# Other halves and other engines for the split of q and k, in an attention and expert kernel

## The chip, the cores and the metric

The kernel runs on one core of one Trainium2 chip. The metric is the device time of one execution, in microseconds (us). A core has five engines that run side by side, each with a queue of its own that it works off in order: TensorE (PE, with its weight loads shown as PEld), VectorE (DVE), ScalarE (ACT), GpSimd (POOL) and SyncE (SP), which here only issues DMAs. An instruction that waits holds up everything behind it in its queue.

## The reference

Eight batches of eight heads of causal attention with a bias that grows with the distance, and then a layer of eight experts, of which each token takes the best one:

```python
scores = scale * np.matmul(q, k.transpose(0, 1, 3, 2))          # 8, 8, 576, 64
cum = np.cumsum(np.maximum(s, 0.0), axis=-1)
bias = -(cum[:, :, :, None] - cum[:, :, None, :])
scores = np.where(causal, -1000000000.0, scores + np.minimum(bias, 0.0))
attn = softmax(scores);  x = (attn @ v), as 4608 tokens x 512
logits = x @ w_gate + modality_bias[modality_id];  e_idx = argmax(logits)
for e in range(E):                                               # 8 experts
    h = np.maximum(x[e_idx == e] @ w1[e], 0.0)                   # 512 -> 1024
    out[e_idx == e] = gate_w[...] * (h @ w2[e])                  # 1024 -> 512
```

## The kernel before

*Pairs.* The attention runs over 32 pairs: one head in two batches (`ab` or `a` = 0 and 1). Eight pairs make a group, which holds all heads of two batches. q and k lie transposed, 64 rows of the head's dimension, and the host writes each of them twice, into partitions 0 to 63 and 64 to 127.

*The split of q and k.* Matmuls run on `F32R`, which keeps fewer bits than float32, so q and k are cut into a high part (the value cast to `F32R`) and a low part (what is left). A score is two matmuls into one tile `sp`: line 288 multiplies `QH` (q's high part in both halves of the partitions) with `KA` (k's high part in one half and its low part in the other), and line 289 multiplies `QL` with `KB`: q's low part with k's high part in partitions 0 to 63, and in further partitions the bias, as rows that `place` brings in by DMA.

*Preparing a pair* (`prep`, lines 223 to 251) is a generator, advanced once in each step of the pair before. Before the change POOL makes the high parts `QH`, `KA` and `KB` (line 233), KA's low part in partitions 64 to 127 (line 248) and QL for `a` = 1 (line 250), DVE makes QL for `a` = 0 (line 239). The first pair has a version of its own, `prep0`.

*A step.* `run` goes through nine steps in a pair, for items in the order 3, 7, 2, 6, 8, 1, 5, 0, 4. Items 0 to 3 are the query blocks of the first batch, of 128 to 512 keys, 4 to 7 those of the second, and 8 holds the last 64 queries of both. A step issues an item's score on PE, its minimum with the mask on DVE (line 291, or 305 for item 8), the exponential on ACT (line 311), and, three steps later, the transposes on PE (line 321) with the copy of the result into `PT` on ACT (line 324) or, for the items in `PTDVE`, on DVE (line 340). The transposes have two buffers, `pt`. `tail` multiplies `PT` with v (`o`, line 361), copies `o` to `oT` on ACT and DVE (lines 364 and 368), multiplies with the gate's weights beside an identity (`ox`, line 255) and scales into `x` and `xq` on DVE (lines 383 and 385).

*Between.* After a group, `Route.group` finds each token's expert on DVE, and POOL scatters nine blocks of rows into `lists` by indirect DMA (line 610), one every `SCS` steps. The third group also computes the first tables of the expert stage. At steps of `setup` constants are written and the bias rows `ek` and `eq` are saved to memory (`save`), from where the pairs from 8 on load them. Each pair's step 7 loads q, k and v of the pair after the next; the buffers are two for q and k, three for v. A planner orders the instructions by their place in the program and by when it thinks them ready; `issue_after` puts an instruction behind another on its engine.

*After.* The expert stage works on blocks of 256 tokens, with weights split in the same way.

Of the kernel before, what the change touches and what calls it, by code (L numbers as in the profile page):

```python
# [7 lines left out]
F32 = mybir.dt.float32  # L8
# [3 lines left out]
AF = mybir.ActivationFunctionType  # L12
ALU = mybir.AluOpType
# [4 lines left out]
P = 128  # L18
KW = 576
XW = 72  # L20
# [7 lines left out]
SPB = 4  # L28
PTDVE = (8,)
QUIET = (6, 7, 8)  # L30


class Attn:

    def __init__(self, ctx, tc, qkv, s, ident):
# [34 lines left out]
        zz = t1.tile([P, 1], F32, name="zz")  # L72
        nc.vector.memset(zz, 0.0)
        for c in range(4):
            nc.vector.memset(ek.bitcast(F32)[:, c, P * (c + 1):], 0.0)
        ho = self.hot(t1)
        nc.vector.tensor_scalar(sr, sr, 0.0, 8.0, ALU.max, ALU.mult)
        cum = [self.ps1.tile([P, 512], F32, name="sp", bufs=SPB) for _ in range(2)]
        nc.vector.tensor_tensor_scan(cum[0], sr[:, :512], zz.broadcast_to([P, 512]), 0.0, ALU.add, ALU.add)
        nc.vector.tensor_tensor_scan(cum[1][:, :64], sr[:, 512:], zz.broadcast_to([P, 64]), cum[0][:, 511:512], ALU.add, ALU.add)  # L80
        nb = t1.tile([P, 5], F32, name="nb")
        nc.vector.tensor_scalar(nb[:, :4], cum[0][:, 0:512:P], -1.0, None, ALU.mult)
        nc.vector.tensor_scalar(nb[:, 4:], cum[1][:, :1], -1.0, None, ALU.mult)
        ekf = ek.bitcast(F32)
        up = slice(64, P)
        for c in (3, 2, 1, 4, 0):
            n = min(P * (c + 1), KW)
            with self.tc.issue_after(self.act):
                for g in range(2 if c == 4 else 1):
                    k = slice(512 * g, min(n, 512 * g + 512))  # L90
                    w = k.stop - k.start
                    i = nc.scalar.activation(ek[:, c, k], cum[g][:, :w], AF.Identity, bias=nb[:, c:c + 1])
                    lo = nc.vector.scalar_tensor_tensor(ek[up, c, k], cum[g][up, :w], nb[up, c:c + 1], ekf[up, c, k], ALU.add, ALU.subtract)
        self.act = i.ins
        with self.tc.issue_after(self.act):
            self.prep0(raw, 0)

        dg = ekf.rearrange("p c k -> p (c k)")
        with self.tc.issue_after(self.act), self.tc.issue_after(lo.ins):
            for ab in range(2):  # L100
                copy = nc.scalar.copy if ab else nc.vector.tensor_copy
                for u in range(2):
                    r = slice(64 * u + 32 * ab, 64 * u + 32 * ab + 32)
                    copy(eq[r, 64 * ab:64 * ab + 512].rearrange("p (c q) -> p c q", c=4),
                         dg[r, :2816].rearrange("p (c x) -> p c x", c=4)[:, :, :P])
                    copy(eq[r, 512 * (1 - ab):512 * (1 - ab) + 64], dg[r, 2816:])
            self.prep0(raw, 1)
            self.rows(ho, 1)
        for pi in range(2):
            self.place(pi)  # L110

    def save(self):

        nc = self.nc
        self.ekd = self.dr.tile([64, 2, 5 * KW], F32, name="ekd")
        self.eqd = self.dr.tile([64, 2, KW], F32, name="eqd")
        for u in range(2):
            r = slice(64 * u, 64 * u + 64)
            nc.sync.dma_start(self.ekd[:, u], self.ek.bitcast(F32)[r].rearrange("p c k -> p (c k)"))
            nc.sync.dma_start(self.eqd[:, u], self.eq.bitcast(F32)[r])  # L120

    def hot(self, t1):

        nc = self.nc
# [8 lines left out]
        self.rows(ho, 0)  # L133
        with self.tc.issue_after(i.ins):
# [18 lines left out]
    def prep0(self, raw, part):  # L153

        nc = self.nc
        rq, rk = raw
        QH, QL, KA, KB = self.QH[0], self.QL[0], self.KA[0], self.KB[0]
        QHf, KAf = QH.bitcast(F32), KA.bitcast(F32)
        lo, up = slice(0, 64), slice(64, P)
        if part:  # L160
            nc.scalar.copy(QH[:, 1, :KW], rq[:, 1])
            nc.scalar.copy(KB[lo, 1], rk[lo, 1])
# [6 lines left out]
        nc.scalar.copy(KA[:, 1], rk[:, 1])  # L169
        nc.scalar.copy(KB[lo, 0], rk[lo, 0])  # L170
        self.last = nc.gpsimd.tensor_tensor(KA[up, 1], rk[up, 1], KAf[up, 1], ALU.subtract).ins

# [21 lines left out]
    def consts(self):  # L194
        nc = self.nc
        for u in range(2):
            nc.gpsimd.memset(self.oT[u][:, 512:], 0.0)
        for t in self.PT:
            nc.vector.memset(t[64:, PTW - 64:], 0.0)
        nc.gpsimd.memset(self.pw, 0.0)  # L200
        for ab in range(2):
            rows = slice(64 * ab, 64 * ab + 64)
            idv = self.ident[rows, 64 * ab:64 * ab + 64]
            nc.scalar.copy(self.pw[rows, :, XW * ab:XW * ab + 64], idv.unsqueeze(1).broadcast_to([64, 8, 64]))
            nc.scalar.copy(self.pq[rows, :, :64], idv.unsqueeze(1).broadcast_to([64, 8, 64]))

# [11 lines left out]

    def load(self, pi):
        self.raw[pi] = self.load_qk(pi)  # L220
        self.V[pi] = self.load_v(pi)

    def prep(self, pi):
        nc = self.nc
        rq, rk = self.raw.pop(pi)
        QH, QL, KA, KB = (t[pi % 2] for t in (self.QH, self.QL, self.KA, self.KB))
        QHf, KAf = QH.bitcast(F32), KA.bitcast(F32)
        if pi > 1:
            self.place(pi)

        def high(o, i):
            with self.tc.issue_after(self.last):
                self.last = nc.gpsimd.tensor_scalar(o, i, 1.0, 1.0, ALU.mult, ALU.mult).ins  # L233

        lo, up = slice(0, 64), slice(64, P)
        for a in range(2):
            high(QH[:, a, :KW], rq[:, a])
        with self.tc.issue_after(self.hold[0]):
            nc.vector.tensor_tensor(QL[lo, 0, :KW], rq[lo, 0], QHf[lo, 0, :KW], ALU.subtract)
        yield  # L240
        for a in range(2):
            high(KA[:, a], rk[:, a])
        yield
        for a in range(2):
            high(KB[lo, a], rk[lo, a])
            yield
        for a in range(2):
            self.last = nc.gpsimd.tensor_tensor(KA[up, a], rk[up, a], KAf[up, a], ALU.subtract).ins  # L248
            yield
        self.last = nc.gpsimd.tensor_tensor(QL[lo, 1, :KW], rq[lo, 1], QHf[lo, 1, :KW], ALU.subtract).ins  # L250
        yield

# [135 lines left out]
    def run(self, npair, newx, done, setup):  # L388
# [5 lines left out]
        for k in range(n + LAG + 9):  # L394
            if k < n:
# [38 lines left out]
def pack(q, k, v, s):  # L434
# [17 lines left out]
    ss = s.reshape(4, 2, 8, 576).transpose(1, 0, 2, 3).reshape(64, 576)  # L452
    return np.ascontiguousarray(out), np.ascontiguousarray(ss)

# [7 lines left out]
PRI2 = 250  # L462
SCS, XB = 4, 4
NRA, NRB = 2, 4
# [8 lines left out]
class Route:  # L473
# [83 lines left out]
    def group(self, bp, x, psum, mm, then=None):  # L557
# [51 lines left out]
        for t in range(9):  # L609
# [4 lines left out]
            self.scat.append(i)  # L614
            for _ in range(SCS):
                yield False
# [393 lines left out]
def build(tc, qkv, s, mid, wg, mb, w1, w2, out):  # L1010
    nc = tc.nc
    with ExitStack() as ctx:
# [9 lines left out]
        with ExitStack() as actx:  # L1022
            xps = [xctx.enter_context(tc.tile_pool(name="xp0", bufs=2, side="right"))]
            A = Attn(actx, tc, qkv, s, ident)

# [77 lines left out]
```

## Time and profile before

| | us |
|---|---|
| median of 3 runs | 898.26 (897.01 to 899.95) |
| the profiled execution | 901.84 |
| its span, first to last instruction | 900.1 |

| engine | busy us | share of the span |
|---|---|---|
| PE | 833.4 | 93% |
| PEld | 726.4 | 81% |
| DVE | 633.0 | 70% |
| ACT | 527.3 | 59% |
| POOL | 574.1 | 64% |

The mean granted clock of TensorE is 0.970. Attention ends at about 427 us, and the rest is the expert stage. The profile's rows give line, engine, operation and tiles as output<-inputs, partitions x elements, a count, busy us and mean ns of one, then the idle time of the engine just before these instructions and what ended it. A row of waits says who waited for whom: us in total, times, longest. A row of the timeline begins with start and duration in us, and its bracket gives the idle time just before and what ended it. POOL's spans are rough, and ends of matmuls are modelled.

### The profile page before, as it was taken

The numbers are of one execution on the slowest core, as the hardware profiler recorded it, in microseconds if no ns is written. First come the engines' busy times: TensorE is split into PE (matmuls) and PEld (weight loads), VectorE is DVE, ScalarE is ACT, GpSimd is POOL, SyncE is SP. The second block draws the span as 40 slices with busy tenths as digits, with TensorE's granted clock in tenths as the row PEclk, the third lists the DMA queues.
The fourth block names the chain that finished last, engine by engine and source line by source line (L and its number), as shares of the span: only waits on it lengthen the run. The fifth ranks groups of instructions, "written<-read, shape, count | busy, mean of one in ns | idle before, by whom it ended". The sixth has DMA issues, their size and how long they took to land. (4 is left out here: it accounts for less than half of the span.)

```text
span 900.1 us, 16902 instructions
## 1 busy us (share of the span) xinstructions
PE 833.4 (93%) x5648; PEld 726.4 (81%) x5648; DVE 633.0 (70%) x1543; ACT 527.3 (59%) x1221; POOL 574.1 (64%) x471
## 2 busy tenths in 40 slices
PE   2889999997999899898989799999999999999984
PEld 2778888876887688686889698999999999999962
DVE  7668788877878688967748866666665666656681
ACT  5757888775877577677545244455554544444541
POOL 7767777778768787772556256565555655545860
PEclk9989999998999899989999999999999999999987
DMA  4563444534445444534878376666666666665840
GB/s 166 162 170 120 161 140 141 186 120 163 140 167 161 142 140 141 191 107 165 312 265 309 133 271 230 238 234 237 237 236 237 237 237 237 237 235 220 294 160 3
DMA packets 68888, 172.85 MB, mean 192 GB/s; under 512 B 13247, under 2 KB 13247, under 8 KB 68672
## 3 DMA queue, kind: packets, MB, share of 16 engines
q1 hardware_dynamic: 62944, 151.70, 48.8%
q0 software_dynamic: 5856, 20.06, 5.7%
q8 instruction: 45, 0.74, 0.3%
q14 instruction: 43, 0.35, 0.1%
HBM read 144.75 MB, written 26.80 MB: 191 GB/s over the span
## 5 line engine op out<-in xcount | busy, mean ns | idle before, releaser
L311 ACT ACTIVATE pe<-pe,mx 128x512 f32<-128x512 f32 (+3 forms) x256 | 143.5, 563 | 29.7 <-DVE mx L291 28.1
L291 DVE CUSTOM_DVE_ANT_0 pe<-sp,mk 128x512 f32<-128x512 f32 (+3 forms) x256 | 120.8, 485 | 28.1 <-PE sp L289 26.4
L324 ACT COPY PT<-pt 128x512 f32<-128x512 f32 (+3 forms) x256 | 104.4, 420 | 53.1 <-PE pt L321 50.1
L907 ACT ACTIVATE hT<-hp 128x512 fp32r<-128x512 f32 x72 | 42.8, 594 | 151.7 <-PE hp L905 147.9
L891 POOL DMA_INDIRECT out<-ys,oi x36 | 40.8, 1133 | 131.8 <-DVE ys L890 49.8
L321 PE MATMUL pt<-ident,pe 128*128 128x128 f32 x640 | 120.3, 287 | 1.5 <-ACT PT L324 1.5
L288 PE MATMUL sp<-KA,QH 128*128 128x256 f32 (+2 forms) x256 | 105.7, 416 | 15.2 <-POOL KA L168 10.4
L361 PE MATMUL o<-PT,V 128*64 128x320 f32 (+4 forms) x896 | 109.7, 373 | 3.5 <-DVE PT L340 3.4
L361 PEld LDWEIGHTS o<-PT,V 128*64 128x64 f32 x896 | 81.7, 140 | 36.4 <-DVE PT L340 15.8
L248 POOL TENSOR_TENSOR KA<-rawk,KA 64x576 fp32r<-64x576 f32 x62 | 88.0, 1434 | 24.9 <-DMA lists<-x,di 19.1
L905 PE MATMUL hp<-xT,wcb 128*128 128x256 f32 x648 | 90.0, 283 | 0.9 <-DVE hT L908 0.9
L321 PEld LDWEIGHTS pt<-ident,pe 128*128 128x128 f32 x640 | 78.9, 147 | 13.3 <-issue 5.6
L289 PE MATMUL sp<-KB,QL 76*128 76x256 f32 (+2 forms) x256 | 88.3, 347 | 0.8 <-POOL QL L250 0.7
L908 DVE SCALAR_TENSOR_TENSOR hT<-hp,hT 128x512 fp32r<-128x512 f32 x72 | 49.3, 684 | 53.0 <-ACT hT L907 52.9
L905 PEld LDWEIGHTS hp<-xT,wcb 128*128 128x128 f32 x648 | 83.5, 189 | 1.7 <-DVE hT L908 1.1
L905 PE MATMUL hp<-xT,wcc 128*128 128x256 f32 x528 | 76.5, 286 | 5.5 <-DVE hT L908 3.1
L884 PE MATMUL y<-wcb,hT 128*128 128x512 f32 x336 | 81.0, 398 | 0.0
L233 POOL TENSOR_SCALAR QH<-rawq 128x576 fp32r<-128x576 f32 x62 | 41.2, 682 | 60.5 <-issue 42.5
L905 PE MATMUL hp<-xT,wca 128*128 128x256 f32 x552 | 78.4, 285 | 0.4 <-ACT xT L870 0.3
L905 PEld LDWEIGHTS hp<-xT,wcc 128*128 128x128 f32 x528 | 69.6, 193 | 6.6 <-DVE hT L908 3.3
L884 PEld LDWEIGHTS y<-wcb,hT 128*128 128x128 f32 x336 | 62.9, 189 | 14.6
L905 PEld LDWEIGHTS hp<-xT,wca 128*128 128x128 f32 x552 | 72.2, 191 | 1.3 <-ACT xT L870 0.5
(271 smaller groups left out, 1952.4 us busy)
## 6 DMA issues: line engine op xcount, KB each, us to landing
wrbw<-in_w SPq DMA_DIRECT2D x104, 512.0 KB
wraw<-in_w SPq DMA_DIRECT2D x56, 512.0 KB
rawq<-in_qkv SPq DMA_DIRECT2D x32, 576.0 KB
rawk<-in_qkv SPq DMA_DIRECT2D x32, 576.0 KB
xg<-lists SPq DMA_DIRECT2D x18, 576.0 KB
V<-in_qkv SPq DMA_DIRECT2D x32, 320.0 KB
lists<-z SPq DMA_DIRECT2D x8, 576.0 KB
ekd<-ek SPq DMA_DIRECT2D x2, 720.0 KB
```

The costliest lines, as they stand in the source:

```text
L248: self.last = nc.gpsimd.tensor_tensor(KA[up, a], rk[up, a], KAf[up, a], ALU.subtract).ins
L288: self.pe.append(nc.tensor.matmul(sp[:, :nn], QH[:, q0:q0 + P], KA[:, ab, :nn], start=True, stop=False).ins)
L289: self.pe.append(nc.tensor.matmul(sp[:, :nn], QL[:EXT, q0:q0 + P], KB[:EXT, ab, :nn], start=False, stop=True).ins)
L291: ins = nc.vector.tensor_tensor_reduce(out=t[:, :n], in0=sp[:, :n], in1=self.mk[:, 512 - n:512], scale=-0.125, scalar=3.0e38, op0=ALU.add, ...
L311: self.act = nc.scalar.activation(t[:, :n], t[:, :n], AF.Exp, bias=m, scale=-1.0, accum_out=st["sums"][:, o:o + 1]).ins
L321: self.pe.append(nc.tensor.transpose(out=pt[:, P * j:P * j + P], in_=pe[:, P * j:P * j + P], identity=self.ident).ins)
L324: cp(w[:, :, v:v + P], pt[:, :P * (c + 1)].rearrange("p (j q) -> p j q", q=P))
L361: m = nc.tensor.matmul(o[r, f - q0:q1 - q0], V[:, ab, j, :], PT[ab][:, PTS * j + f if j < 4 else PTW - 64:PTS * j + q1 if j < 4 else PTW], ...
L884: self.last[0] = nc.tensor.matmul(y[u], hT[:, a, f, P * u:P * u + P], W[4 + f // 2][:, c, 512 * (f % 2):512 * (f % 2) + 512], start=f == 0 ...
L905: nc.tensor.matmul(hp[:, u], W[k][:, a, f:f + P], xT[:, c, k], start=k == 0 and i == 0, stop=k == 3 and i == 2)
L907: nc.scalar.activation(hs, hp, AF.Relu)
L908: nc.vector.scalar_tensor_tensor(hT[:, 1, 2 * m:2 * m + 2], hp, 0.0, hs.bitcast(F32), ALU.max, ALU.subtract)
```

## The change

- `prep`: KA's conversion for both `a` goes from POOL to ACT, behind the latest exponential. KA's low part goes from partitions 64 to 127 into 0 to 63 (the high part stands in the other half, so the products are the same), and both low parts of q are made on POOL. The order is now QH, KB, QL, and KA last.
- `PTDVE` is (2, 6, 8) in place of (8): the copies of items 2 and 6 go from ACT to DVE.
- `SCS` is 5 for the first two groups and stays 4 for the others.
- v of a pair is loaded at step 2 of the pair before; before, it was loaded five steps and a whole pair earlier, at step 7. `save` writes the halves at steps 17 and 26 and no longer both at 17.
- The start: `s` comes doubled from the host in one DMA; ACT does its maximum and scale, in two parts; the scan is in three parts; ACT copies the upper half of the sums into a tile `cl`, from which DVE makes the low parts of `ek`; all of the first pair's KA is made on POOL; the rows `eq` are all copied by ACT; `pw` and `pq` (identity and gate's weights) are filled at the start and no longer at steps 5 and 8.

```diff
-PTDVE = (8,)
+PTDVE = (2, 6, 8)
-SCS, XB = 4, 4
+SCS = 5, 5, 4, 4
...
     def __init__(self, ctx, tc, qkv, s, ident, wg):
-        for u in range(2):
-            nc.sync.dma_start(sr[64 * u:64 * u + 64], s)
+        nc.sync.dma_start(sr, s)
         raw = self.load_qk(0)
-        self.load(1)
-        self.V[0] = self.load_v(0)
+        self.raw[1] = self.load_qk(1)
+        for pi in range(2):
+            self.V[pi] = self.load_v(pi)
...
-        nc.vector.tensor_scalar(sr, sr, 0.0, 8.0, ALU.max, ALU.mult)
+        nc.vector.memset(self.pw, 0.0)
+        self.unit(self.pq, 0)
+        self.setup(wg)
+        for k in (slice(0, 256), slice(256, KW)):
+            i = nc.scalar.activation(s8[:, k], sr[:, k], AF.Relu, scale=8.0)
+        with self.tc.issue_after(i.ins):
+            self.rows(ho, 0)
...
+        cl = self.ps1.tile([P, 512], F32, name="pt")
+        with self.tc.issue_after(self.act):
+            i = nc.scalar.copy(cl[up], cum[0][up])
+        self.act = i.ins
...
-                    lo = nc.vector.scalar_tensor_tensor(ek[up, c, k], cum[g][up, :w], ...)
+                    lo = nc.vector.scalar_tensor_tensor(ek[up, c, k], (cum[1] if g else cl)[up, :w], ...)
...
+        own(0, 0); own(0, 1)                      # eq's rows, all on ACT
+        for ab in range(2):
+            own(1, ab)
+            self.prep0(raw, 1 + ab)               # KB on ACT, QL on DVE
+        self.place(0)
+        self.rows(ho, 1)
+        self.unit(self.pw, XW)
+        self.place(1)
...
+    def unit(self, t, w):
+        for ab in range(2):
+            rows = slice(64 * ab, 64 * ab + 64)
+            self.act = self.nc.scalar.copy(t[rows, :, w * ab:w * ab + 64], self.ident[rows, 64 * ab:64 * ab + 64]...).ins
...
     def prep0(self, raw, part):
-        nc.gpsimd.tensor_scalar(QH[:, 0, :KW], rq[:, 0], 1.0, 1.0, ALU.mult, ALU.mult)
-        nc.gpsimd.tensor_scalar(KA[:, 0], rk[:, 0], 1.0, 1.0, ALU.mult, ALU.mult)
-        nc.gpsimd.tensor_tensor(KA[up, 0], rk[up, 0], KAf[up, 0], ALU.subtract)
-        nc.scalar.copy(KA[:, 1], rk[:, 1])
...
+        for a in range(2):
+            nc.gpsimd.tensor_scalar(QH[:, a, :KW], rq[:, a], 1.0, 1.0, ALU.mult, ALU.mult)
+            nc.gpsimd.tensor_scalar(KA[:, a], rk[:, a], 1.0, 1.0, ALU.mult, ALU.mult)
+            self.last = nc.gpsimd.tensor_tensor(KA[lo, a], rk[lo, a], KAf[lo, a], ALU.subtract).ins
...
     def prep(self, pi):
+        def low(o, i, h):
+            with self.tc.issue_after(self.last):
+                self.last = nc.gpsimd.tensor_tensor(o, i, h, ALU.subtract).ins
         for a in range(2):
             high(QH[:, a, :KW], rq[:, a])
-        with self.tc.issue_after(self.hold[0]):
-            nc.vector.tensor_tensor(QL[lo, 0, :KW], rq[lo, 0], QHf[lo, 0, :KW], ALU.subtract)
-        yield
-        for a in range(2):
-            high(KA[:, a], rk[:, a])
         yield
         for a in range(2):
             high(KB[lo, a], rk[lo, a])
+        yield
+        for a in range(2):
+            low(QL[lo, a, :KW], rq[lo, a], QHf[lo, a, :KW])
             yield
         for a in range(2):
-            self.last = nc.gpsimd.tensor_tensor(KA[up, a], rk[up, a], KAf[up, a], ALU.subtract).ins
+            with self.tc.issue_after(self.act):
+                self.act = nc.scalar.copy(KA[:, a], rk[:, a]).ins
+            low(KA[lo, a], rk[lo, a], KAf[lo, a])
             yield
-        self.last = nc.gpsimd.tensor_tensor(QL[lo, 1, :KW], rq[lo, 1], QHf[lo, 1, :KW], ALU.subtract).ins
-        yield
...
     def run(self, npair, newx, done, setup):
+                if k % 9 == 2 and 0 < pi < npair - 1:
+                    self.V[pi + 1] = self.load_v(pi + 1)
                 if k % 9 == 7 and pi + 2 < npair:
-                    self.load(pi + 2)
+                    self.raw[pi + 2] = self.load_qk(pi + 2)
...
-            for _ in range(SCS):
+            for _ in range(SCS[bp]):
                 yield False
...
-            setup = {5: A.consts, 7: R.consts, 8: lambda: A.setup(wg), 17: A.save, 20: lambda: R.setup(mid, mb, A.t1p)}
+            setup = {5: A.consts, 7: R.consts, 17: lambda: A.save(0), 26: lambda: A.save(1), 20: lambda: R.setup(mid, mb, A.t1p)}
```

More of the change, by code (lines that the diff above doesn't have):

```diff
@@ L28, with __init__ @@
 SPB = 4
-PTDVE = (8,)
+PTDVE = (2, 6, 8)
 QUIET = (6, 7, 8)
 class Attn:
-    def __init__(self, ctx, tc, qkv, s, ident):
+    def __init__(self, ctx, tc, qkv, s, ident, wg):
         nc = tc.nc
@@ L109, in __init__ @@
-        for pi in range(2):
-            self.place(pi)
-    def save(self):
-        nc = self.nc
[L115 to L120, printed above, removed]
+                    lo = nc.vector.scalar_tensor_tensor(ek[up, c, k], (cum[1] if g else cl)[up, :w], nb[up, c:c + 1], ekf[up, c, k], ALU.add, ALU.subtract)
@@ new lines, in __init__, with own @@
+            self.act = i.ins
+        self.prep0(raw, 0)
+        dg = ekf.rearrange("p c k -> p (c k)")
+        up = slice(64, P)
+        def own(u, ab):
+            with self.tc.issue_after(self.act):
+                r = slice(64 * u + 32 * ab, 64 * u + 32 * ab + 32)
+                nc.scalar.copy(eq[r, 64 * ab:64 * ab + 512].rearrange("p (c q) -> p c q", c=4),
+                               dg[r, :2816].rearrange("p (c x) -> p c x", c=4)[:, :, :P])
+                self.act = nc.scalar.copy(eq[r, 512 * (1 - ab):512 * (1 - ab) + 64], dg[r, 2816:]).ins
@@ new lines, in __init__ @@
+        own(0, 0)
+        own(0, 1)
+        self.hold[0] = lo.ins
+        for ab in range(2):
+            own(1, ab)
+            with self.tc.issue_after(self.act), self.tc.issue_after(self.hold[0]):
+                self.prep0(raw, 1 + ab)
+        self.place(0)
+        with self.tc.issue_after(self.act):
+            self.rows(ho, 1)
+        with self.tc.issue_after(self.act):
+            self.unit(self.pw, XW)
[3 more added lines that the diff above has]
+            rows = slice(64 * ab, 64 * ab + 64)
+            self.act = self.nc.scalar.copy(t[rows, :, w * ab:w * ab + 64], self.ident[rows, 64 * ab:64 * ab + 64].unsqueeze(1).broadcast_to([64, 8, 64])).ins
@@ L199, in consts @@
             nc.vector.memset(t[64:, PTW - 64:], 0.0)
[L200 to L205, printed above, removed]
     def load_qk(self, pi):
```

49 lines of the change are left out of this document (21 added, 28 removed).

## The prediction

> **What bounds the kernel now.** I read the stages first (busy time by stretch), then the time of each pair of heads, then the waits, then the instructions around the longest waits. The first row below shows all engines from pair 4 to pair 11 (us, busy us and count of PE, PEld, DVE, ACT, POOL, granted clock, DMA share, GB/s), the second the expert stage. The others count the `xq` instruction of line 385, which runs once in a pair: each row is a stretch cut just before one such instruction, its length, and how many pair lengths it holds.
>
> ```profile
> 77.40:166.90 89.50, 89.30 (x708) 78.42 (x707) 73.25 (x291) 72.15 (x229) 67.84 (x72) 1.00 0.45 153
> 427.00:880.00 453.00, 441.57 (x2794) 395.97 (x2793) 298.98 (x335) 217.73 (x274) 260.04 (x121) 0.98 0.65 239
> ```
> ```profile
> 37.70:64.30 26.60, 0.57 (x2) 0.94 0.66 146
> 64.30:77.40 13.10, 0.28 (x1) 0.86 0.43 140
> 77.40:166.90 89.50, 2.27 (x8) 1.00 0.45 153
> 166.90:223.60 56.70, 1.14 (x4) 0.94 0.47 154
> ...
> 268.50:323.50 55.00, 1.14 (x4) 0.94 0.49 158
> ...
> 356.90:397.90 41.00, 0.85 (x3) 0.92 0.46 156
> ```
>
> In an undisturbed stretch PE is busy 89.30 of 89.50 us, and a pair takes 89.5 / 8 = 11.19 us: PE is the bound. The expert stage is PE's too (441.57 of 453). The disturbed stretches are the loss: pairs 12 to 15 take 56.7 - 4 x 11.19 = 11.9 us more, pairs 20 to 23 10.2, pairs 27 to 29 41.0 - 33.6 = 7.4, pairs 1 to 3 39.7 - 33.6 = 6.1. In them the clock is lower as well, which is in these lengths. Three of the four are the stretches in which POOL scatters the rows of a finished group:
>
> ```profile
> POOL KA L248 <- DMA lists<-x,di: 19.1, 11, 2.1
> POOL KA L248 <- DMA lists<-xq,di: 4.0, 2, 2.0
> DVE QL L239 <- POOL QH L233: 17.3, 8, 4.4
> POOL QH L233 <- DMA rawq<-in_qkv: 8.2, 1, 8.2
> PEld o L361 <- DVE PT L340: 15.8, 33, 1.7
> ```
> ```profile
> 184.99 1.05 POOL L610 DMA_INDIRECT lists<-x,di  x1 [0.28 <-POOL KA L248]
> 186.11 1.40 POOL L250 TENSOR_TENSOR QL<-rawq,QH 64x576 fp32r<-64x576 f32 x1
> ...
> 196.59 1.05 POOL L610 DMA_INDIRECT lists<-x,di  x1 [0.28 <-POOL KA L248]
> 199.54 1.41 POOL L248 TENSOR_TENSOR KA<-rawk,KA 64x576 fp32r<-64x576 f32 x1 [1.91 <-DMA lists<-x,di]
> 201.03 1.40 POOL L250 TENSOR_TENSOR QL<-rawq,QH 64x576 fp32r<-64x576 f32 x1
> ```
> ```profile
> 204.35 3.09 DVE L239 TENSOR_TENSOR QL<-rawq,QH 64x576 fp32r<-64x576 f32 x1 [4.41 <-POOL QH L233]
> ```
> ```profile
> 207.87 0.70 PE L255 MATMUL ox<-pq,oT 128*128 128x72 f32 x2 [4.39 <-DVE oT L368]
> ```
>
> This is the chain of a disturbed pair. POOL does 67.84 / 8 = 8.48 us of preparation in a pair; a scatter every four of nine steps adds 2.25 x (1.05 + 0.2) = 2.8; and KA's low part (line 248, partitions 64 to 127) stands waiting for a scatter to land, 23.1 us over some 12 pairs, 1.9 in each. That is 13.2, over PE's 11.19, so POOL falls behind from pair to pair. DVE's QL of line 239 waits for POOL's QH; behind it in DVE's queue stands `oT` of line 368, and PE waits for that.
>
> **The change part by part.** Durations, by shape:
>
> ```profile
> L248 POOL TENSOR_TENSOR KA<-rawk,KA 64x576 fp32r<-64x576 f32 x62 | 88.0, 1434 | 24.9 <-DMA lists<-x,di 19.1 <-DMA lists<-xq,di 4.0
> L250 POOL TENSOR_TENSOR QL<-rawq,QH 64x576 fp32r<-64x576 f32 x31 | 44.5, 1437 | 2.4
> L233 POOL TENSOR_SCALAR KA<-rawk 128x576 fp32r<-128x576 f32 x62 | 46.3, 761 | 0.2
> L239 DVE TENSOR_TENSOR QL<-rawq,QH 64x576 fp32r<-64x576 f32 x31 | 36.8, 1188 | 17.3 <-POOL QH L233 17.3
> L324 ACT COPY PT<-pt 128x384 f32<-128x384 f32 x64 | 27.4, 478 | 0.0
> L340 DVE COPY PT<-pt 128x256 f32<-128x256 f32 x64 | 24.1, 416 | 2.4 <-PE pt L334 2.2
> L169 ACT CAST KA<-rawk 128x576 fp32r<-128x576 f32 x1 | 0.7, 661 | 0.0
> ```
>
> *Work of a pair.* POOL loses two KA conversions (2 x 0.76) and gains the second QL (1.44): 8.48 becomes 8.40. ACT gains two KA conversions (2 x 0.66) and loses two PT copies (2 x 0.48): 72.15 / 8 = 9.02 becomes 9.38. DVE loses QL (1.19) and gains two PT copies of 128x384. No row has that on DVE; 1.5 times the 128x256 row is 0.62, and two reads of line 340 in a row pace at 0.38 each (0.76 for two, below), which gives 0.47 to 0.57; I take 0.55. 73.25 / 8 = 9.16 becomes 9.07. No engine's sum reaches 11.19; what counts is the place in the queue.
>
> *DVE no longer waits for POOL.* With line 239 gone from DVE, the 17.3 us have no instruction left to stand on.
>
> *KA's low part in partitions 0 to 63, scatters every 5 steps in the first two groups.* QL's low part (line 250) is the same operation on the same shape in partitions 0 to 63, and it has no wait for a scatter in any row: at 186.11 it starts 0.07 us behind one, while KA's at 199.54 waits 1.91. I take the wait as tied to the upper partitions and gone. Then a pair of the scatter stage costs POOL 8.40 + 9/5 x 1.25 = 10.7, under PE; in the third group (still every 4 steps) 8.40 + 2.8 = 11.2, at the edge. Of 11.9 + 10.2 = 22.1 I take 20 (if the wait stays: 11, see the rivals); of the third's 7.4 I take 4, since its pairs also carry the first routing tables' DVE work, which stays.
>
> The Trainium skill, GPSIMD Engine Reference, section "Extended-addressing connectivity", says that for a tensor_tensor each core works on its own 16 partitions, so that the half in which the operands lie would not matter; by it KA's wait would stay, and the sum would come out at the 889 of the second rival. The two rows above disagree with that reading, so the sum goes by the rows. The same page, section "Engine selection", has two-input elementwise work about twice as slow on GpSimd as on VectorE; by it the second QL would cost 2.4 us, and the third group's pairs 12.2 on POOL, some 2 us more in the sum. The rows have 1437 against 1188 ns for this very operation, a factor 1.21, and the rows decide.
>
> *The price in an undisturbed pair.* It lies where DVE's copies end and the 20 matmuls of `o` begin:
>
> ```profile
> 248.24 0.78 ACT L311 ACTIVATE pep<-pep,mx 128x576 f32<-128x576 f32 x1
> ...
> 248.79 0.42 DVE L291 CUSTOM_DVE_ANT_0 pe<-sp,mk 128x256 f32<-128x256 f32 x1 [0.73 <-PE sp L289]
> ...
> 249.48 0.52 ACT L311 ACTIVATE pe<-pe,mx 128x256 f32<-128x256 f32 x1
> ...
> 251.20 0.76 DVE L340 COPY PT<-pt 128x256 f32<-128x256 f32 x2
> ...
> 251.26 0.48 PE L288 MATMUL sp<-KA,QH 128*128 128x512 f32 x1
> ...
> 251.91 2.23 PEld L361 LDWEIGHTS o<-PT,V 128*64 128x64 f32 x20 [0.37 <-DVE PT L340]
> ```
>
> From 248.79 to 251.96 DVE works almost without a gap, and `o` starts as its last copy ends: 33 of these waits are in the list above. The copies of items 2 and 6 now fall into this stretch, 2 x 0.55 = 1.1. Some of it is covered, since DVE waited for PE before the last copies and two routing instructions of this pair (0.36) are not in most pairs. Bounds 0 and 1.1; I take 0.5, nearer to the middle because the end of the last copy and the start of `o` touch. Over pairs 2 to 31: 30 x 0.5 = +15.0. The second tight place is new: ACT converts KA only behind the exponential of item 8. That ends at 249.1 (0.19 to read the sum stands behind its 0.78); 0.66 and POOL's 1.43 end at 251.2, and the next pair's first score starts at 251.26. I cost it at nothing; whatever ACT does between the two comes out of PE one for one.
>
> *Saves, loads of V.*
>
> ```profile
> 39.56 0.33 SPq L216 DMA_DIRECT2D V<-in_qkv  x1
> ...
> 54.79 0.36 SPq L211 DMA_DIRECT2D rawq<-in_qkv  x1
> ```
>
> SP's load of V for pair 3 stands until 39.56 for a free buffer; behind it come four saves and the bias rows, and rawq of pair 4 is issued only at 54.79. POOL waits 8.2 us for it, and pairs 1 to 3 lose 6.1. Now V is asked for when its buffer has long been free, and half of the saves follow nine steps later, behind the loads. I take -5 (bounds 0 and -6.1; what is late next is `rawq` behind the first half).
>
> *Start.*
>
> ```profile
> L92 ACT ACTIVATE ek<-sp,nb 128x512 fp32r<-128x512 f32 (+4 forms) x6 | 3.0, 517 | 5.4 <-DVE nb L82 2.7 <-DVE ek L93 2.7
> ```
> ```profile
> 17.50 1.09 PE L289 MATMUL sp<-KB,QL 76*128 76x512 f32 x2
> ...
> 26.05 0.60 ACT L204 COPY pw<-ident 64x512 f32<-64x512 f32 x1
> ...
> 27.70 0.61 ACT L205 COPY pq<-ident 64x512 f32<-64x512 f32 x1
> ...
> 28.87 0.66 PE L334 MATMUL pt<-ident,pep 128*128 128x128 f32 x4 [2.87 <-ACT PT L324]
> ```
>
> In the first lines of the kernel ACT (line 92) and DVE (line 93) take turns on the bias rows, each waiting for the other on one tile; ACT loses 2.7 us so. DVE now reads a copy of it in another tile, for which ACT spends some 0.6 us. POOL converts KA itself and no longer waits for ACT there. The first score's second half, at 17.50 now, hangs on both; I take -3, the 2.7 and a little of POOL's (bounds 0 and -5, the DMAs of the rows still coming behind the first loads). The four fills of `pw` and `pq` (2.4 us) leave the place where PE waits 2.87 us for a copy behind them, but two KA conversions (1.3) come in there and two fills run just before the first exponential: -2 (bounds 0 and -2.9). The four loads of the gate's weights move on SP into the time before the bias rows are ready, when SP has nothing to issue; the moved memset and the fills on ACT and DVE lie under the wait for the first loads.
>
> **Sum.** -20 - 4 - 5 - 3 - 2 + 15 = -19. Pair 31 and the expert stage stay. The profiled execution took 901.84 us (span 900.1), 3.6 more than the median of 898.26; from the median the sum gives 879.3, from the profiled one 882.8. I forecast 880.
>
> **The rivals.** *All of DVE's added copies hide*, as PE may have been the later one: the +15 falls away, 864. For it: the 0.73 us that DVE idles at 248.79; against: 15.8 us of waits for line 340 already. *KA's wait stays*, that is, the move to the lower half does not do what it seems to: POOL's pair is 10.7 + 0.85 x 1.8 = 12.2 in ten pairs against 11.7 (+5.5), 13.1 in the third group (+4): 889. For it: the wait is named after the scatter's data, not after a partition; against: line 250. *Slower*: ACT's queue puts the copy of item 7 and the exponential of item 1 (249.48, 0.52 and 0.19) ahead of KA's conversion; then POOL's low part ends 1.24 us later, at 252.5, and each first score with it. 30 x 1.24 = 37 in place of 15: 902. It decides from 0.5 + 19/30 = 1.13 us in a pair. For it: 0.06 us of slack; against: the order of issue puts KA's conversion right behind item 8. *Nothing to tell*: the price is about 1.1 us for other reasons, 898.
>
> **How the numbers follow.** Forecast 0.47, all hidden 0.17, the wait stays 0.16, slower 0.12, no difference 0.08. Faster by over 0.3% (2.7 us, about what a measurement can tell) is 0.47 + 0.17 + 0.16 = 0.80, the same 0.08, slower 0.12. The forecast's own range is 870 to 888 (0.2 to 0.8 us a pair). The range for all reaches to 864 and past 889: 863 to 896, which leaves out the last two cases.
>
> **What would show it.** Right: pairs 12 to 15 and 20 to 23 at 11.5 to 12 us, no row of KA's low part waiting for `lists`, no DVE wait for POOL's QH, the first score's second half at 14 to 15 us, rawq of pair 4 issued by 49. The price shows as `o` waiting for DVE's PT, 0.4 to 0.9 us in nearly each pair, and undisturbed pairs at 11.7. Wrong: undisturbed pairs over 12.3, `sp` waiting for POOL's KA in each pair, or POOL still over 12 us in a scatter pair.

## The result and the profile after

The changed kernel takes 922.01 us (median of four runs, 921.30 to 923.24) against 897.78 us before on the same chip: a ratio of 1.0261, 95% interval 1.0236 to 1.0286. It is 24 us slower, where 880 was forecast. The profiled execution took 922.01 us, with a span of 920.3 and a mean granted clock of 0.978 (0.970 before), so the clock is not the cause.

The lengths of the pairs, read as in the prediction (stretches cut just before an `xq` instruction, now line 403; length first, the number of pairs in the second bracket):

```profile
33.30:72.50 39.20, 0.85 (x3) 0.92 0.54 157
...
84.60:172.70 88.10, 1.98 (x7) 1.00 0.44 141
172.70:226.30 53.60, 1.14 (x4) 0.97 0.50 157
278.90:332.50 53.60, 1.13 (x4) 0.97 0.49 156
370.10:417.20 47.10, 0.85 (x3) 0.96 0.41 136
```

The first `xq` comes 4.4 us earlier than before (33.4 against 37.8), the last one 21.5 us later (444.8 against 423.3), and what follows it is as long as it was. So the whole loss lies in the 31 pairs. The seven pairs from 84.60 on take 12.6 us at the mean, where PE had set 11.2; in that stretch single pairs take 11.6 (pairs 5 to 7 and 9) and others 13.2 to 15.1 (pairs 8, 10, 11). Pairs 12 to 15 fell only from 56.7 to 53.6, and pairs 27 to 29 rose from 41.0 to 47.1.

The longest waits between 30 and 450 us (who waited for whom: us in total, times, longest):

```profile
POOL KA L253 <- ACT KA L267: 114.8, 30, 6.0
DVE oT L386 <- ACT oT L382: 55.4, 29, 4.2
ACT pe L329 <- DVE mx L309: 47.0, 45, 2.7
...
PE o L379 <- DVE PT L358: 20.8, 31, 2.5
```

The largest, POOL waiting for ScalarE's conversion of k, is new and looks like the culprit. The waits for the scatter and DVE's wait for POOL's QH are gone, as forecast. But a list of waits does not show an instruction that has started and does not get on. That is in the durations. First the groups by shape of the kernel before, then those of the changed one:

```profile
L373 DVE TENSOR_TENSOR rs<-sums,eps 128x5 f32<-128x5 f32 x32 | 16.2, 505 | 0.0
...
L374 DVE RECIPROCAL rs<-rs 128x5 f32<-128x5 f32 x32 | 6.1, 191 | 1.0
```
```profile
L391 DVE TENSOR_TENSOR rs<-sums,eps 128x5 f32<-128x5 f32 x32 | 38.4, 1201 | 0.0
...
L391 DVE TENSOR_TENSOR rs<-sums,eps 128x4 f32<-128x4 f32 x32 | 7.0, 219 | 0.0
...
L392 DVE RECIPROCAL rs<-rs 128x5 f32<-128x5 f32 x32 | 6.1, 191 | 1.0
```

`rs<-sums,eps` adds a constant to five numbers in each partition. It takes 1201 ns on average, while the reciprocal of the same five takes 191. No line of it was changed. Its place in pair 12, DVE's queue and then POOL's:

```profile
182.60 0.69 DVE L309 CUSTOM_DVE_ANT_0 pe<-sp,mk 128x512 f32<-128x512 f32 x1
...
183.22 2.91 DVE L391 TENSOR_TENSOR rs<-sums,eps 128x5 f32<-128x5 f32 x1
186.16 0.19 DVE L392 RECIPROCAL rs<-rs 128x5 f32<-128x5 f32 x1
...
187.03 0.55 DVE L309 CUSTOM_DVE_ANT_0 pe<-sp,mk 128x384 f32<-128x384 f32 x1
```
```profile
182.03 1.30 POOL L249 TENSOR_SCALAR KB<-rawk 64x576 fp32r<-64x576 f32 x2
183.30 2.79 POOL L253 TENSOR_TENSOR QL<-rawq,QH 64x576 fp32r<-64x576 f32 x2
```

The addition starts at 183.22 and ends at 186.13, just after POOL's two low parts of q (183.30 + 2.79 = 186.09). Behind it in DVE's queue stands the minimum of the next score, 187.03. In this trace 19 of the 64 additions last over 0.4 us, 37.7 us together, and each ends 0.02 or 0.03 us after a POOL instruction does. In an undisturbed pair the addition falls into the seam between the two low parts and passes (pair 9, DVE, then POOL):

```profile
143.61 0.16 DVE L391 TENSOR_TENSOR rs<-sums,eps 128x5 f32<-128x5 f32 x1
```
```profile
142.28 2.80 POOL L253 TENSOR_TENSOR QL<-rawq,QH 64x576 fp32r<-64x576 f32 x2
```

A few hundredths of a microsecond decide there: in pairs 9, 17 and 25 the addition starts about 0.08 us before the first low part ends, and gets in between the two; in pairs 10, 18 and 26 it starts 0.05 to 0.06 us before that end, and stands through the second. At the seven seams between KB's conversion and the first low part (pair 12 above is one) it never got in.

From pair 8 on, 18 pairs hold such a standing addition, of 1.35 us or more, and these are just the 18 pairs of 12.8 us or more; the other six take 11.3 to 11.6.

### The profile page after: what moved, and what is told of

It is laid out like the page before. It is cut to its first block, busy times and chain, and to the rows that moved or that the text cites. A ratio compares the mean times of both kernels' runs of the same rounds, so it can differ in the third digit from the quotient of the medians.

```text
span 920.3 us, 16918 instructions
## 1 busy us (share of the span) xinstructions
PE 833.0 (91%) x5648; PEld 705.3 (77%) x5648; DVE 639.4 (69%) x1573; ACT 544.4 (59%) x1224; POOL 565.3 (61%) x441
## 5 line engine op out<-in xcount | busy, mean ns | idle before, releaser
L379 PE MATMUL o<-PT,V 128*64 128x320 f32 (+4 forms) x896 | 104.1, 372 | 21.5 <-DVE PT L358 21.1
L306 PE MATMUL sp<-KA,QH 128*128 128x256 f32 (+2 forms) x256 | 102.9, 409 | 14.7 <-POOL KA L197 10.8
L379 PEld LDWEIGHTS o<-PT,V 128*64 128x64 f32 x896 | 60.2, 139 | 66.6 <-DVE PT L358 29.0
L342 ACT COPY PT<-pt 128x512 f32<-128x512 f32 (+2 forms) x192 | 77.6, 405 | 40.1 <-PE pt L339 35.6
L253 POOL TENSOR_TENSOR QL<-rawq,QH 64x576 fp32r<-64x576 f32 x62 | 86.8, 1417 | 0.2
```

The source lines that it names most:

```text
L253: self.last = nc.gpsimd.tensor_tensor(o, i, h, ALU.subtract).ins
L306: self.pe.append(nc.tensor.matmul(sp[:, :nn], QH[:, q0:q0 + P], KA[:, ab, :nn], start=True, stop=False).ins)
L342: cp(w[:, :, v:v + P], pt[:, :P * (c + 1)].rearrange("p (j q) -> p j q", q=P))
L379: m = nc.tensor.matmul(o[r, f - q0:q1 - q0], V[:, ab, j, :], PT[ab][:, PTS * j + f if j < 4 else PTW - 64:PTS * j + q1 if j < 4 else PTW], ...
```

## The experiments

Theory 1: DVE's addition stands while POOL works in SBUF, and this holds up DVE, then ACT and PE. Theory 2: POOL's waits for ACT's conversion of k set the long pairs. Theory 3: the PT copies on DVE do, with the group's DVE work. Each ratio is against the kernel before, measured along with it on the same chip (897.8, 898.2 and 897.9 us).

### The addition left out of the changed kernel

```diff
-            nc.vector.tensor_tensor(rs[:, :n], st["sums"][:, 4 * g:4 * g + n], self.eps[:, :n], ALU.add)
-            nc.vector.reciprocal(rs[:, :n], rs[:, :n])
+            nc.vector.reciprocal(rs[:, :n], st["sums"][:, 4 * g:4 * g + n])
```

> The changed kernel, with one VectorE instruction left out: the addition of 1e-9 to the sums (rs<-sums,eps); the reciprocal reads the sums directly (each sum holds an exp of 0, so it is at least 1). Theory 1, the standing addition: in the changed kernel's trace this addition, 0.16 us at its median, lasts up to 3.1 us where POOL's low parts of q run, and ends 0.02 to 0.03 us after the POOL instruction does; its time above the median is 34.6 us in 64 instructions. Without it pairs 10 to 13, 18 to 21 and 26 to 29 fall from 13-16 us to 11.5-12.5, and the kernel to 882-890 us. Theory 2, ScalarE's conversion of k: POOL's low parts of k wait 120 us for it, and this sets the long pairs; theory 3, the two more PT copies on VectorE are the loss, with the group's VectorE work in the same stretch. By both, the addition is a symptom: one small instruction less is worth at most its 64 x 0.16 = 10 us, most of it not on the path, and the time is 914-922.

Measured: 888.05 us, ratio 0.9897 (0.9861 to 0.9934), as theory 1 had it. 34 us are gone with an instruction whose own work is about 10 us. Its stretches of pairs 12 to 15 and 27 to 29, and the reciprocal that now reads the sums:

```profile
165.10:210.40 45.30, 1.13 (x4) 1.00 0.58 184
...
342.30:386.20 43.90, 0.84 (x3) 0.92 0.43 139
```
```profile
L391 DVE RECIPROCAL rs<-sums 128x5 f32<-128x5 f32 x32 | 5.9, 184 | 0.0
```

Pairs 12 to 15 fall from 53.6 to 45.3 us, all four at 11.33. POOL still waits 93 us for ACT, so by themselves these waits are not the loss. Pairs 9 to 11 stay long (12.1 to 13.1) against the expectation, and so does pair 27, at 17.5 us. There other small DVE instructions of the routing stand as the addition did (DVE's queue, then POOL's):

```profile
352.23 3.27 DVE L667 TENSOR_TENSOR fa<-fexc,numf 128x48 f32<-128x48 f32 x1
...
356.03 2.14 DVE L668 TENSOR_TENSOR foh<-foh,fa 128x48 f32<-128x48 f32 x1
```
```profile
352.75 1.30 POOL L249 TENSOR_SCALAR KB<-rawk 64x576 fp32r<-64x576 f32 x2
354.03 1.40 POOL L253 TENSOR_TENSOR QL<-rawq,QH 64x576 fp32r<-64x576 f32 x1
...
356.69 1.41 POOL L253 TENSOR_TENSOR QL<-rawq,QH 64x576 fp32r<-64x576 f32 x1
```

### The addition kept, with the constant in the instruction

```diff
-            nc.vector.tensor_tensor(rs[:, :n], st["sums"][:, 4 * g:4 * g + n], self.eps[:, :n], ALU.add)
+            nc.vector.tensor_scalar(rs[:, :n], st["sums"][:, 4 * g:4 * g + n], 1.0e-9, None, ALU.add)
```

> The changed kernel, with the addition kept as an instruction of the same size and place, but with the constant as an immediate in place of the tile of constants: one operand in SBUF in place of two. Theory 1, if it is the second SBUF operand that makes the instruction stand: 0.16-0.2 us each, and a time within 3 us of the kernel without the addition (882-893). Theory 1, if any VectorE instruction that works from SBUF to SBUF stands behind POOL: 922, as the changed kernel. Theories 2 and 3: 922 as well.

Measured: 922.81 us, ratio 1.0295 (1.0252 to 1.0339), no better than the changed kernel.

```profile
L391 DVE TENSOR_SCALAR rs<-sums 128x5 f32<-128x5 f32 x32 | 38.4, 1199 | 0.0
```

So it isn't the second operand alone: a DVE instruction with one operand that adds from SBUF to SBUF stands just as long. Not every one does: in the run without the addition 27 of the 64 reciprocals ran wholly inside a POOL instruction and none lasted over 0.19 us, and DVE's minima and copies, which read PSUM, keep their lengths too (the 128x512 minimum 0.67 to 0.69 us in the changed kernel). The Trainium skill, page "SBUF — State Buffer", section "SBUF: two separate sides", has the rule: VectorE and GpSimd share one pair of SBUF ports as an exclusive lock that whoever starts first holds for its whole instruction, and VectorE needs it with two SBUF inputs (against a GpSimd instruction that reads SBUF) or in a mode that uses two ports for one input. The ends of the standing additions agree with it (0.02 to 0.03 us behind POOL's). That the one-operand form is in such a mode would explain this run; no run here shows the mode itself.

### The addition left out of the kernel before

The same edit in the kernel before.

> The kernel before, with the same addition left out. Theory 1: in its trace the addition has 18.8 us above its median of 0.23, most of it in pairs 12 to 15, 20 to 23 and 27 to 29, the pairs that the prediction put down to POOL's subtraction behind the scatter: the time falls to 881-890. If the prediction was right that the scatter's waits make these pairs long, the addition waits beside them and costs nothing: 895-898.

Measured: 900.49 us, ratio 1.0034 (1.0015 to 1.0054): nothing gained, and a little over both expectations. By the two traces, pairs 12 to 15, 20 to 23 and 27 to 29 get 6.9 us shorter, as theory 1 had it, and pairs 8 to 11, 16 to 19 and 24 to 26 get 7.7 us longer: in these, other instructions now stand (pair 10, 13.0 us instead of 11.3; DVE's queue, then POOL's):

```profile
155.94 1.34 DVE L583 TENSOR_SCALAR gs<-gs 128x9 f32<-128x9 f32 x1
```
```profile
154.46 2.79 POOL L248 TENSOR_TENSOR KA<-rawk,KA 64x576 fp32r<-64x576 f32 x2
```

So the removal of a standing instruction, though in sight, need not gain anything: what follows it moves too and can meet POOL in its turn. That it was worth 0 here and 34 us there was not to be read from its duration alone.

### k's low part in partitions 0 to 63, alone, in the kernel before

```diff
-            self.last = nc.gpsimd.tensor_tensor(KA[up, a], rk[up, a], KAf[up, a], ALU.subtract).ins
+            self.last = nc.gpsimd.tensor_tensor(KA[lo, a], rk[lo, a], KAf[lo, a], ALU.subtract).ins
```

(and the same in `prep0`)

> The kernel before with one part of the change alone: the subtraction of k's low part on GpSimd works in partitions 0 to 63 instead of 64 to 127. By the prediction's step for the scatter stages this takes away POOL's 13 waits for the scatter (23.1 us), and pairs 12 to 15, 20 to 23 and 27 to 29 fall from 12.4-16.3 us towards 11.2-12: 870-880 us. If those waits have a cause other than the partitions, or lie beside another wait that is as long: 895-900. If POOL, no longer held up, brings its subtractions under VectorE's addition of the constant (theory 1): part of it is lost, 880-893.

Measured: 914.28 us, ratio 1.0196 (1.0161 to 1.0231).

```profile
L248 POOL TENSOR_TENSOR KA<-rawk,KA 64x576 fp32r<-64x576 f32 x62 | 89.2, 1455 | 0.1
...
L373 DVE TENSOR_TENSOR rs<-sums,eps 128x5 f32<-128x5 f32 x32 | 37.6, 1176 | 0.0
```

This is the change in small. The waits of KA's low part go from 24.9 us to 0.1, as forecast, and the kernel gets slower by 16 us: POOL, not held up any more, does its subtractions without a gap, and the additions rise from 505 to 1176 ns. The expectation named that loss, but at about half its size: none of its three ranges has the kernel slower than before.

The same without the addition:

> The same with the addition of 1e-9 left out (the reciprocal reads the sums directly). By theory 1 it shows what the partitions alone are worth when the addition can't stand behind POOL: 868-882 if the scatter's waits set the long pairs of before, 897-902 if they don't. Its difference to the run with the addition is what the additions cost there.

Measured: 895.11 us, ratio 0.9979 (0.9959 to 0.9998). The additions cost 19 us of the 914. The time lies between the two expectations. Against the kernel before without the addition (900.5) the partitions bring 5 us, much less than the first of them: pairs 12 and 13 fall to 10.96 us, but pairs 23 and 28 take 16.3 and 17.8. In pair 23 DVE's own low part of q, still there in this kernel, stands (DVE's queue, then POOL's):

```profile
302.00 7.32 DVE L239 TENSOR_TENSOR QL<-rawq,QH 64x576 fp32r<-64x576 f32 x1
309.24 0.45 DVE L368 COPY oT<-o 64x64 f32<-64x64 f32 x2
```
```profile
302.06 1.30 POOL L233 TENSOR_SCALAR KA<-rawk 128x576 fp32r<-128x576 f32 x2
303.34 1.29 POOL L233 TENSOR_SCALAR KB<-rawk 64x576 fp32r<-64x576 f32 x2
304.61 2.74 POOL L248 TENSOR_TENSOR KA<-rawk,KA 64x576 fp32r<-64x576 f32 x2
307.31 1.39 POOL L250 TENSOR_TENSOR QL<-rawq,QH 64x576 fp32r<-64x576 f32 x1
```

It starts at 302.00 and ends 0.62 us after the last of seven POOL instructions that follow each other without a gap. So here the wait was for the end of the string, not of one instruction. A lock that is held for one instruction does not explain that by itself; why DVE gets in at some seams of such a string and not at others is not shown.

### k's first conversion back on GpSimd, without the addition

```diff
-            with self.tc.issue_after(self.act):
-                self.act = nc.scalar.copy(KA[:, a], rk[:, a]).ins
+            high(KA[:, a], rk[:, a])
             low(KA[lo, a], rk[lo, a], KAf[lo, a])
```

> The changed kernel without the addition (888 us), and k's first conversion on GpSimd again, right ahead of each subtraction. POOL's waits for ScalarE, 93 us in the run without the addition, go, and POOL has 2 x 0.66 us more in each pair, ScalarE as much less. Theory 2 (those waits set the pairs): 870-880. If the waits cost nothing and ScalarE is what bounds the calm pairs: 11.33 us falls to about 11.0, 878-884. If POOL's added work counts (its scatter pairs had 9.4-10.3 us busy of 11.3-15): 895-910.

Measured: 883.32 us, ratio 0.9838 (0.9805 to 0.9870). That is 4.7 us under the run without the addition; calm pairs are as before at 11.31, and the gain lies at the start (first `xq` at 31.55 instead of 33.11, pair 1 at 11.3 instead of 12.9) and in the group's pairs (pairs 9 to 11 take 36.3 us instead of 38.0, pairs 27 to 29 42.5 instead of 43.9). The time lies in the range 878-884, but for another reason than the one given there (calm pairs at 11.0). In this kernel the 93 us of waits thus cost 4.7 us: they are not the loss of 34, and theory 2 falls.

### The scatters 4 steps apart, without the addition

```diff
-SCS = 5, 5, 4, 4
+SCS = 4, 4, 4, 4
```

> The changed kernel without the addition (888 us), and the scatters of the first two groups 4 steps apart again instead of 5. The prediction gave this edit nothing: 886-890. If the wider spacing is what keeps the scatter pairs short (11.33 us in pairs 12 to 15 and 20 to 23 there): 892-900.

Measured: 887.70 us, ratio 0.9891 (0.9868 to 0.9914), the 888 of the run without this edit. The spacing does nothing in this kernel; whether it does with the loop of before, no run shows.

### k's first conversion back on GpSimd, with the addition

The edit that gave k's first conversion back to GpSimd, in the changed kernel itself, addition kept.

> The changed kernel (922 us) with one edit undone: k's first conversion is on GpSimd again, right ahead of each subtraction; VectorE's addition of the constant is kept. Without the addition this edit was worth 4.7 us (888.1 to 883.3). If POOL's waits for ScalarE are what puts the low parts of q under the addition, the collisions go: 884-895. If POOL's chain of instructions without a gap collides as much or more (before with the partitions alone changed had 36.0 us of standing additions and 914 us): 910-930.

Measured: 905.57 us, ratio 1.0084 (1.0056 to 1.0113), between the two expectations. It gains 16 us on the changed kernel, but the addition still costs 22 (905.6 against 883.3). ScalarE's conversion thus was one reason why POOL's work met the addition, and not the only one: here it stands behind KA's subtractions and conversions as well.

### The PT copies of items 2 and 6 back on ScalarE

```diff
-PTDVE = (2, 6, 8)
+PTDVE = (8,)
```

In the changed kernel, then without the addition, and without the addition and with k's conversion on GpSimd:

> The changed kernel with the PT copies of items 2 and 6 on ScalarE again (only item 8's on VectorE). The price that the prediction gave these copies is 0.5 us in each of 30 pairs: calm pairs 11.6 to 11.15, in sum 13-15 us, so 907-909 by theory 1 if the collisions of the addition stay as they are, between 890 and 912 since their places shift. Theory 3: the loss goes altogether, 875-885.

> The changed kernel without the addition (888 us), with the PT copies of items 2 and 6 on ScalarE again. With the addition this edit cost 22 us, calm pairs 12.80 us instead of 11.62. If ScalarE, with k's conversion and four more copies, is what bounds these pairs: 12.6-12.8 us a pair again, 31 x 1.3 = 40 us more, 920-930. If the loss there was collisions: 885-892. By the prediction's price (0.5 us a pair for having them on VectorE): 872-876.

> The changed kernel without the addition, k's first conversion on GpSimd (883 us), and the PT copies of items 2 and 6 on ScalarE, which then has the work per pair that it had before. By the prediction's price, calm pairs fall from 11.31 us by 0.45-0.5 to the 10.9 us that the kernel before without the addition has, 31 x 0.4 = 12 us: 868-873. If the copies are free on VectorE: 882-885. If ScalarE bounds even without the conversion: 890-900.

Measured: 944.22 us, ratio 1.0519 (1.0481 to 1.0556); 912.75 us, ratio 1.0171 (1.0116 to 1.0226); 872.56 us, ratio 0.9717 (0.9673 to 0.9762). The first went against both theories that it was to tell apart, the second lies outside its three ranges, and the third came as forecast by the prediction's price. Together the last two show what the first could not. Two calm pairs of the second and of the third kernel (busy us and count of PE, PEld, DVE, ACT, POOL):

```profile
94.93:119.26 24.33, 23.85 (x176) 19.10 (x175) 14.74 (x63) 19.67 (x61) 16.25 (x17) 1.00 0.47 155
```
```profile
87.65:109.54 21.89, 21.89 (x176) 18.06 (x175) 14.56 (x63) 17.98 (x57) 18.95 (x21) 1.00 0.60 208
```

In the third, PE is busy all the time and a pair takes 10.95 us. With the copies on DVE it takes 11.31 (883.3 us in all): the price of the copies is 0.36 us a pair, 10.8 us in all. In the second, ACT has the copies and k's conversion: 12.16 us a pair, 40 us more than the third. ACT is busy 19.67 of 24.33 us there, so its sum is not too large. But in the first of these pairs it works without a pause up to 103.6 us, with both conversions in the middle (98.12 and 99.93), and its 2.2 us of idle time all lie behind that. I read this as the place of the conversion in its queue; no run moved it there. Hence the copies' move to DVE is a loss of 11 us where GpSimd converts k, and a gain of 25 where ScalarE does. The third kernel is the fastest of all: 25 us under the kernel before, 49 under the changed one. Its stretches of pairs 1 to 3, 12 to 15 and 27 to 29:

```profile
31.30:65.00 33.70, 0.85 (x3) 1.00 0.63 173
...
156.80:201.40 44.60, 1.14 (x4) 1.00 0.55 171
...
327.30:370.20 42.90, 0.85 (x3) 0.92 0.45 149
```

### The start alone

The changed kernel with `prep` and `PTDVE` as in the kernel before; the start, the loads of v, the saves and the spacing as changed.

> The changed kernel's start, its later loads of v, its saves in parts and its spacing of the scatters, with the loop's conversions, low parts and PT copies as in the kernel before (addition kept). The prediction's terms for these edits are 3 + 2 + 5 = 10 us: 886-890. If the loop gives the gain of the start back (other places of the same instructions in the scatter stages): 893-900.

Measured: 887.42 us, ratio 0.9877 (0.9837 to 0.9916): -10.5 us, the 10 that the prediction's three terms had. Its parts are not those of the forecast: by the traces the first `xq` comes 6.2 us earlier (5 forecast), pairs 1 to 3 take 2.9 us less (5 forecast), and pairs 12 to 15 and 20 to 23 together 7.8 us less, while the profiled execution of before was itself some 4 us over the median. This run has the wider spacing as well, and no run has the start without it.

## Why the prediction was wrong

From the kernel before, through the start alone and the fastest kernel, to the changed one the steps are: 897.9 - 10.5 (start, saves, v, spacing) - 14.9 (k's low part in the lower partitions, q's both on GpSimd, and no addition) + 10.8 (copies on DVE) + 4.7 (k's conversion on ScalarE) + 34.0 (the addition) = 922.0. Each step is the difference of two runs, so they must add up. Their sizes depend on the order in which the edits are made, as the copies show.

- **What failed: the addition is not in the prediction.** The step "DVE no longer waits for POOL" says that with line 239 gone the 17.3 us have no instruction left to stand on. That looked at DVE's waits for POOL's results, and not at DVE's work beside POOL's. The 505 ns beside the reciprocal's 191 stood in the view by shape from which the prediction took its durations. The sum had 0 for it, the runs have 34 us, and no rival had it. The slower rival was another mechanism (ACT's queue ahead of KA's conversion, 902). Without the addition the changed kernel takes 888.05, the upper end of the forecast's own range of 870 to 888.
- **The same was in the prediction's row for line 239, misread.** Its 1188 ns are not the instruction's own work. In the trace of before, 27 of its 31 executions end 0.60 to 0.62 us after a POOL conversion or subtraction that ran beside them. The one at 204.35, shown in the prediction with its 3.09 us, stood through these (POOL's queue):

```profile
203.62 1.32 POOL L233 TENSOR_SCALAR QH<-rawq 128x576 fp32r<-128x576 f32 x2
204.90 1.29 POOL L233 TENSOR_SCALAR KA<-rawk 128x576 fp32r<-128x576 f32 x2
206.17 1.79 POOL L233 TENSOR_SCALAR KB<-rawk 64x576 fp32r<-64x576 f32 x2
```

The first of the two KB conversions ends at 206.83, QL at 207.44, and the two conversions take 1.79 us instead of 1.30: the second in its turn lasts longer beside QL. From these ends I estimate QL's own work on DVE at 0.6 us. So the factor between GpSimd and VectorE is about 2.4 (1437 ns to 600), nearer to the "about twice" that the prediction set aside than to its 1.21. The sum took POOL's 1.44 and is not changed by it, but half of the row's time was a wait of the kind that then cost 34 us.

- **Scatter stages, -20 and -4.** The mechanism was right: the waits go when the partitions change alone, and in the fastest kernel, without the addition, pairs 12 to 15 take 44.6 us instead of 56.7, 12.1 less, a little more than the whole excess of 11.9 that the prediction saw there; pairs 20 to 23 take 44.2 instead of 55.0. Not all of it is the partitions: with the start alone these eight pairs are already 7.8 us shorter, and the step behind it brings 14.9 us where the prediction had 24. The -4 for the third group failed: 42.9 us against 41.0. In pair 28 of that kernel a subtraction of six numbers per partition, of the first tables' work, lasts 3.49 us (DVE's queue):

```profile
350.19 3.49 DVE L720 TENSOR_TENSOR fs<-numf,fs 128x6 f32<-128x6 f32 x1
```

The prediction's figures for the case that KA's wait stays do not agree with each other: 11 of the 20 left in this step, 14.5 (20 less 5.5) in the rival, whose 889 would be 892 by the first. The wait went, so nothing hangs on it. What a POOL without waits does next, string its instructions together, was not asked: the prediction looked for what is late next among those who wait for POOL, not on the engine beside it.

- **Copies on DVE, +15.** The size was near (+10.8), and the place right: `o` waits 20.8 us in 31 waits for the last copy. But it holds only where GpSimd converts k. In the changed kernel, where ScalarE does, the copies on DVE gain 22 us (25 without the addition): there the sign was wrong.
- **KA's conversion on ACT, at nothing.** Without the addition it costs 0 in calm pairs and 4.7 us in all with the copies on DVE, 40 with the copies on ACT; with the addition and the copies on DVE, 16. With both on ACT a calm pair is 1.21 us longer, near to the 1.32 of the two conversions, which fits "one for one". Copies and conversion together are 15.5 us, by luck almost the 15 of the two terms.
- **Start -3, second part -2, saves and v -5.** Right together, -10.5, but in part by luck, as the run of the start alone shows. v of a pair is asked for four steps later than before (step 2 of the pair before it in place of step 7 of the pair before that), and not five steps and a whole pair as said under the change. The first score's second half starts at 15.74 instead of 17.50, a little late for the forecast, and q of pair 4 is issued at 48.13 instead of 54.79 (PE's row, then SP's):

```profile
15.74 0.77 PE L307 MATMUL sp<-KB,QL 76*128 76x512 f32 x1 [2.75 <-DMA QL<-eq]
```
```profile
48.13 0.37 SPq L231 DMA_DIRECT2D rawq<-in_qkv  x1
```

- **Signs named ahead.** Calm pairs at 11.6 (11.7 named), no wait of KA for `lists` and none of DVE for QH, as named for "right"; three of the four pairs 12 to 15 at 13.0 to 15.3 us instead of 11.5 to 12, POOL's busy time in them 9.7 to 11.7, under the 12 that was to show "wrong". One sign for "wrong" did come: the seven pairs 5 to 11, undisturbed before, take 12.6 us at the mean, over the 12.3 that was named, though the calm ones among them take 11.6. The others watched POOL's sum and the waits, and the loss was in neither.

Left open: why in just these pairs the addition misses the seam. That its length depends on what POOL does beside it is shown by the runs that shift POOL's work (505, 1176, 1201 ns for the same instruction); what sets the phase in each pair was not traced. That the port lock is what makes it stand is argued from these ends and the rule quoted above; the runs show only that it ends with POOL's instructions. That the routing's instructions in pairs 27 and 28 cost what they stand for is read from the trace alone; no run removed them.

## What to carry to other kernels

Before moving work between GpSimd and VectorE, look in the view by shape for tiny VectorE instructions that last far longer than their neighbours of the same shape, and find whose end theirs falls on: waits that no list shows. The mean of such a row is not an instruction's own work; here 1188 ns were 600 and a wait. Freeing an engine of its waits also changes what it collides with, so ask not only who waits for it but which engine it shares something with. And price two edits that load the same queue together, since each alone may cost nothing, or have the other sign.

## What was not expected of the hardware

- An addition of five numbers per partition on VectorE, 0.16 us alone, lasted up to 3.1 us beside GpSimd's subtractions; a subtraction of 64x576 whose own work is about 0.6 us (the estimate above) lasted 7.32 beside seven GpSimd instructions in a row, one-input casts among them.
- A reciprocal from SBUF to SBUF of the same size did not stand (184 ns at the mean), while an addition with an immediate did (1199 ns). Leaving the addition out, not rewriting it, was the cure.
- The same GpSimd subtraction has 24.9 us of waits, 23.1 of them behind an indirect scatter, in partitions 64 to 127, and 0.1 us in partitions 0 to 63. Why is not shown.
